# Attention steps between triples of the experts' products, with an order edge two steps back

## The chip, the cores and the metric

The kernel runs on one NeuronCore of a Trainium2 chip. The metric is the device time of one execution in microseconds (us); less is better. The engines are TensorE (PE in the rows; PEld is its loading of weights), VectorE (DVE), ScalarE (ACT), GpSimd (POOL) and SyncE (SP, which issues DMAs).

## What is computed

An attention over 2 x 8 heads of 576 positions and 64 features, with a causal mask and a bias from a running sum of `s`; then a mixture of four experts with dense weights (every token goes through every expert); then a gated layer. All of it is float32.

```python
def _attn_ref(q, k, v, s):                      # q, k, v: 2 x 8 x 576 x 64
    scores = np.matmul(q, k.transpose(0, 1, 3, 2)) / np.sqrt(D)
    cum = np.cumsum(np.maximum(s, 0.0), axis=-1)
    bias = -(cum[:, :, :, None] - cum[:, :, None, :])
    scores = np.where(causal, -1e9, scores + np.minimum(bias, 0.0))
    attn = np.exp(scores - np.max(scores, axis=-1, keepdims=True))
    attn = attn / (np.sum(attn, axis=-1, keepdims=True) + 1e-09)
    return np.matmul(attn, v)

def _moe_ref(x, domain_probs, w1, w2):          # x: 1152 x 512, four experts, F = 1024
    p = domain_probs / (domain_probs.sum(-1, keepdims=True) + 1e-09)
    for e in range(E):
        out += p[:, e:e + 1] * (np.maximum(x @ w1[e], 0.0) @ w2[e])

def _moe2_ref(x, w_a, w_b, w_out):              # F = 1536
    return ((x @ w_a) * (x @ w_b)) @ w_out
```

## The kernel before

Every float32 matrix is split into a high and a low part, and a product of two of them is a **triple** of matmuls, high x high, high x low and low x high, which the helper `mm3` (lines 255 to 261) issues to TensorE. All expert products therefore carry line 259 in the profile. An **attention step** works on the tiles of scores of 128 query rows: there are 80 such tiles in four groups (`GROUPS`: group 0 has 16 tiles, groups 1 and 2 have 24 each, group 3 has 16), and `attn_step` (line 792) is a software pipeline over them. In step n it issues, in this order, the transposes of tile n-3 (line 644), the score matmuls of tile n (lines 596 and 597), the normalisation of tile n-2 (ScalarE line 631, VectorE line 632, GpSimd line 633), the maximum and exponential of tile n-1 (VectorE line 606, ScalarE line 621), the P·V product of a head that is complete (line 680), and the evacuation of the transposes (ScalarE line 659 for the high part, VectorE line 661 for the low part). The first step of a head also prepares the next head (`prep_job`, among it the low half of k on GpSimd, line 564) and issues the loads of the head after that.

The work has three parts. First group 0 is done alone with the first weights being loaded (to about 38 us). Then `run(beside, True)` lays the experts' products of four stages beside the steps of groups 1 to 3: a stage is an expert and a range of 256 tokens, with eight first-layer units (`l1_unit`: four triples of 256 columns) and two second-layer units (`l2_unit`: eight triples of 512 columns); `pipelined` puts one first-layer unit of the next stage before the two second-layer units of a stage. Last, `run(after, False)` does the remaining experts and the gated layer without attention, with other pools of memory; its products write the tile psq.

What sets the order in the middle part: `run` keeps a clock `clock["t"]` of product time by a formula of the kernel, 3 x (columns / 2400 + 0.013) us for a triple, which is 0.36 us for 256 columns and 0.68 us for 512. After each unit it emits weight steps (a weight piece is loaded into `raw`, rounded by ScalarE at line 218 and its rest taken by GpSimd or VectorE at line 220) until their own clock has caught up, and then as many attention steps as the list `lead` asks for: steps 20 to 43 (group 1) in the first 29.7 us of product time, steps 44 to 67 in the next 22.35 us, steps 68 to 83 in the next 22.35 us; the last 15 us (`SLACK`) have none. Steps 0 to 19 have been emitted before the loop. The order on each engine is drawn from this program order at compile time: an instruction of lower place in the program goes first when a modelled run finds it ready; where it is not ready, a later one may pass it. On the chip each engine then takes its instructions in that order.

Of the kernel before, what the change touches and what calls it, by code (L numbers as in the profile page):

```python
# [19 lines left out]
P = 128  # L20
# [26 lines left out]
NT0 = 256  # L47

NFIRST = 4


@with_exitstack
def fused_kernel(ctx, tc, qT, kT, v, s, dp, w1, w2, wa, wb, wo, out):
    nc = tc.nc
# [13 lines left out]
    ident = const.tile([P, P], F32, name="ident")  # L68
# [3 lines left out]
    def split(hi, lo, src, lo_eng):  # L72
        nc.scalar.activation(out=hi, in_=src, func=AF.Copy)  # L73
        lo_eng.tensor_tensor(out=lo, in0=src, in1=hi.bitcast(F32), op=ALU.subtract)  # L74
# [117 lines left out]
    def split_piece(r, key, form, wide, src, j):  # L192
# [16 lines left out]
        else:  # L209
            nsplit[0] += 1  # L210
            lo_eng = nc.gpsimd if nsplit[0] % 2 or nsplit[0] <= NFIRST else nc.vector
            two = slice(2 * j, 2 * j + 2)
            if nsplit[0] <= NFIRST:
                nc.gpsimd.tensor_scalar(
# [37 lines left out]
    hts = {}  # L252
    begun = set()

    def mm3(ps, w, x, first, last, more=False):

        (lh, ll), (rh, rl) = w, x
        for k, (l, r) in enumerate(((lh, rh), (lh, rl), (ll, rh))):
            nc.tensor.matmul(  # L259
                ps, lhsT=l, rhs=r, start=first and k == 0, stop=last and k == 2, skip_group_check=more  # L260
            )

    def cols(pair, *at):
        return tuple(t[(slice(None), *at)] for t in pair)
# [316 lines left out]
    def st_enter(j, i):  # L581
        j.t[i] = Job()
        j.t[i].n = j.tiles[i][0] + P

    def st_scores(j, i):
        t = j.t[i]
        q0 = j.tiles[i][0] - j.q0
        cuts = [0, t.n] if t.n <= 512 else [0, 320, t.n]
        t.ps = []
        for c0, c1 in zip(cuts, cuts[1:]):  # L590
            ps = ps_s.tile([P, c1 - c0], F32, tag="sc", name=f"sc{j.nm}_{i}")
            t.ps.append((ps, c0, c1))
            if j.gi == 0:
                nc.tensor.matmul(ps, lhsT=j.qh[:, q0 : q0 + P], rhs=j.kr[:, c0:c1], start=True, stop=True)
                continue
            nc.tensor.matmul(ps, lhsT=j.qh[:, q0 : q0 + P], rhs=j.ks[:, c0:c1], start=True, stop=False)
            nc.tensor.matmul(ps, lhsT=j.qb[:, q0 : q0 + P], rhs=j.kb[:, c0:c1], start=False, stop=True)

    def st_softmax(j, i):
        t = j.t[i]  # L600
# [36 lines left out]
    def st_transpose(j, i):  # L637
        t = j.t[i]
        t.tp = []
        for c0, c1 in [(0, i + 1)] if i < 4 else [(0, 4), (4, 5)]:  # L640
            ps = ps_t.tile([P, c1 - c0, P], F32, tag="tr", name=f"tr{j.nm}_{i}")
            for c in range(c0, c1):
                k0 = j.tiles[c][0]
                nc.tensor.transpose(ps[:, c - c0, :], t.e[:, k0 : k0 + P], ident)  # L644
            t.tp.append((ps, c0, c1))

    def st_evac(j, i):
        t = j.t[i]
        if i == j.i0:

            j.eh = et_p.tile([P, j.i1, j.nr], F32R if j.gi else F32, tag="eh", name=f"eh{j.nm}")
            if j.gi:
                j.el = et_p.tile([P, j.i1, j.nr], F32R, tag="el", name=f"el{j.nm}")
        w0, r0, r1 = j.tiles[i]
        x = slice(r0 - j.r0, r1 - j.r0)
        for ps, c0, c1 in t.tp:
            src = ps[:, :, r0 - w0 : r1 - w0]
            hi = j.eh[:, c0:c1, x]
            nc.scalar.activation(out=hi, in_=src, func=AF.Copy)
            if j.gi:  # L660
                nc.vector.tensor_tensor(  # L661
                    out=j.el[:, c0:c1, x], in0=src, in1=hi.bitcast(F32), op=ALU.subtract
                )
        del j.t[i]
# [3 lines left out]
    def st_av(j):  # L668
        a = (j.h % 2) * D
        if j.gi == 0 and j.h % 2:  # L670
            ps = xpair[j.gi]
        else:
            ps = ps_a.tile([P, j.nr], F32, tag="av", name=f"av{j.nm}")
        mms = []
        for c in range(j.i1):
            o = max(0, j.tiles[c][1] - j.r0)
            for e in (j.eh, j.el) if j.gi else (j.eh,):
                mms.append((c, o, e))
        for m, (c, o, e) in enumerate(mms):
            nc.tensor.matmul(  # L680
                ps[:, o:] if j.gi else ps[a : a + D, o:],
                lhsT=j.vs[:, c, :],
                rhs=e[:, c, o:],
                start=(m == 0),
                stop=(m == len(mms) - 1),
            )
        c = D - a
        t0 = j.b * S + j.r0
        x = slice(t0, t0 + j.nr)
        if j.gi == 0:  # L690
            xpair[j.gi] = ps
            if j.h % 2:
                split(xh[j.h // 2][:, x], xl[j.h // 2][:, x], ps, nc.vector)
            return
        if j.h % 2 == 0:
            xpair[j.gi] = (
                x_p.tile([P, j.nr], F32, tag="xs", name="xs"),
                x_p.tile([P, j.nr], F32, tag="xt", name="xt"),
            )
        xs, xt = xpair[j.gi]  # L700
        nc.scalar.activation(out=xt[a : a + D, :], in_=ps[c : c + D, :], func=AF.Copy)
        nc.vector.tensor_tensor(  # L702
            out=xs[a : a + D, :], in0=ps[a : a + D, :], in1=xt[a : a + D, :], op=ALU.add
        )
        if j.h % 2 == 1:
            split(xh[j.h // 2][:, x], xl[j.h // 2][:, x], xs, nc.gpsimd)
# [8 lines left out]
    c0 = st_p.tile([NR, 1], F32, tag="c0", name="c0")  # L715
# [70 lines left out]
    state = {"n": 0}  # L786
    prep_job(jobs[0])

    def at(n):
        return seq[n] if 0 <= n < len(seq) else None  # L790

    def attn_step():
        n = state["n"]
        state["n"] += 1

        if x := at(n):
            j, i = x
            if i == j.i0:
                k = jobs.index(j)
                if k + 1 < len(jobs):  # L800
                    prep_job(jobs[k + 1])
                if k + 2 < len(jobs):
                    load_job(jobs[k + 2])
            st_enter(j, i)
        if x := at(n - 3):
            st_transpose(*x)
        if x := at(n):
            st_scores(*x)
        if x := at(n - 2):
            st_norm(*x)  # L810
        if x := at(n - 1):
            st_softmax(*x)
        if x := at(n - 4):
            j, i = x
            if i == j.i1 - 1:
                st_av(j)
        if x := at(n - 3):
            st_evac(*x)
        if x := at(n):
            j, i = x  # L820
            if i == j.i0:
                prep_v(j)
                k = jobs.index(j)
                if k + 1 < len(jobs):
                    load_v(jobs[k + 1])
# [6 lines left out]
    def close_attention():  # L832
        actx.close()
        open_pools(ctx, [("h2", 2), ("raw", 3), ("q", 2), ("cv", 1)])
        pools["late"] = True
        late_ps.append(ctx.enter_context(tc.tile_pool(name="ps_m2", bufs=5, space=PSUM)))
        for part_ in ("h", "l"):
            tq[part_] = ctx.enter_context(tc.tile_pool(name="tq" + part_, bufs=1)).tile(
                [P, 3, 2, SL], F32R, name="tq" + part_
            )  # L840
# [211 lines left out]
    n = [k for k, u in enumerate(after) if u[0] == ("w1", halves[1][1])][-1]  # L1052
# [11 lines left out]
    area = [0]  # L1064
# [5 lines left out]
    for n in (2, 3, 4):  # L1070
        us = sum(c for st in stages[:n] for part in expert_stage(*st) for _, c, _ in part)
        turn_t.append(us)
    SLACK = 15.0
    lead = []
    for g in range(3):
        u0 = lead[-1][1] if lead else 0.0
# [2 lines left out]
    PACE, LATE_PACE = 4.0, 3.0  # L1079
    clock = {"t": 0.0, "w": 0.0}  # L1080

    def run(units, attention):
        for k, cost, u in units:
            for key in keys_of(k):
                weights_to(key)
            u()
            for key in keys_of(k):
                used(key)
            if hold[0]:
                continue  # L1090
            clock["t"] += cost
            while clock["w"] < clock["t"]:
                clock["w"] += PACE if attention else LATE_PACE
                weight_step()
            if not attention:
                continue
            goal = state["n"]
            for u0, u1, s0, s1 in lead:
                if u0 < clock["t"]:
                    c = area[s0] + (area[s1] - area[s0]) * min(1.0, (clock["t"] - u0) / (u1 - u0))  # L1100
                    while goal < s1 and area[goal + 1] <= c + 1e-6:
                        goal += 1
            while state["n"] < goal:
                attn_step()

    run(beside, True)
    close_attention()
    run(after, False)


# [48 lines left out]
```

## Time and profile before

| | |
|---|---|
| Time, median of 3 runs | 761.77 us (760.43 to 764.9) |
| Time of the profiled execution | 760.76 us |
| Its span, from the first to the last instruction | 759.0 us |
| Mean granted clock of TensorE in it | 0.987 |
| TensorE busy | 719.9 us (95%) |
| VectorE busy | 533.0 us (70%) |
| GpSimd busy | 416.2 us (55%) |
| ScalarE busy | 334.8 us (44%) |

The times are of whole executions; the profile is one of them, taken by the hardware profiler, and all rows below are from it, in us from its first instruction. An engine's busy time is the union of its instructions' spans. A matmul's span includes its way through the array, so the next one starts before it ends: the distance between two starts is what a matmul costs, not its span. PEclk is the granted clock of TensorE as a share of the full one: 1.00 is 2.4 GHz and 0.50 is 1.2 GHz, and values between are means over a stretch.

### The profile page before, as it was taken

What the parts mean: (1) busy time and instruction counts of PE and PEld (TensorE: products, weight loads), DVE (VectorE), ACT (ScalarE), POOL (GpSimd) and SP (SyncE); (2) the same over time, 40 slices, a digit from 0 to 9 for tenths busy, and PEclk for the clock granted to TensorE, in tenths of its full rate; (3) what the DMA queues carried; (4) which work ended last, traced back from release to release, by engine and by line L of the source; (5) the groups of instructions that cost most, each with busy time, mean ns of one, the idle gap of its engine ahead of it and who ended that gap; (6) DMA issues with size and microseconds to landing.
All of it is one profiled execution on the core that took longest, in us unless ns stands there. A gap on an engine that the chain in (4) does not pass through costs nothing.

```text
span 759.0 us, 11106 instructions
## 1 busy us (share of the span) xinstructions
PE 719.9 (95%) x3868; PEld 630.9 (83%) x3868; DVE 533.0 (70%) x1119; ACT 334.8 (44%) x756; POOL 416.2 (55%) x330
## 2 busy tenths in 40 slices
PE   5979897997998999999999999999899999999997
PEld 3678886886978888888888888888788888898896
DVE  7656857757759777776556657679874788887764
ACT  4667748868864432223312323243645324242410
POOL 1777735647634754333313344598466878788600
PEclk9999998999998999999999999999999999999999
DMA  6457323324402131211001112122102132213003
GB/s 192 136 184 228 91 68 90 100 74 127 120 18 84 55 100 41 81 57 57 31 25 56 56 57 74 65 84 87 53 29 86 62 103 68 95 63 104 5 1 125
DMA packets 35095, 61.34 MB, mean 81 GB/s; under 512 B 3472, under 2 KB 19376, under 8 KB 35040
## 3 DMA queue, kind: packets, MB, share of 16 engines
q1 hardware_dynamic: 34864, 60.50, 24.8%
q8 instruction: 31, 0.51, 0.3%
q14 instruction: 24, 0.20, 0.1%
q10 hardware_dynamic: 176, 0.14, 0.1%
HBM read 55.02 MB, written 2.58 MB: 76 GB/s over the span
## 4 chain that ended last, share of the span: by engine, by line
PE 55%; DVE 12%; POOL 8%; issue 4%; ACT 2%; DMA 1%; POOLq 0%; ACTq 0%; DVEq 0%; SPq 0%
PE ps L259 27%; PE psq L259 20%; PE pst L259 4%; POOL wl L74 3%; PE av L680 2%; POOL tp L155 1%; DVE tp L167 1%; PE tr L644 1%; DVE tp L163 1%; DVE h2l L74 1%; DVE acc L1027 1%; DVE tp L159 1%; POOL t L155 1%; DVE t L167 1%; DVE psq L405 1%
## 5 line engine op out<-in xcount | busy, mean ns | idle before, releaser
L259 PE MATMUL ps<-wh,h2h 128*128 128x512 f32 x332 | 130.6, 393 | 0.0
L259 PE MATMUL ps<-wl,h2h 128*128 128x512 f32 x332 | 129.6, 390 | 0.0
L74 POOL TENSOR_TENSOR wl<-raw,wh 128x1024 fp32r<-128x1024 f32 x24 | 58.5, 2448 | 125.5 <-ACT wh L73 95.4
L259 PE MATMUL ps<-wh,h2l 128*128 128x512 f32 x332 | 125.7, 392 | 0.8 <-DVE h2l L74 0.8
L307 DVE SCALAR_TENSOR_TENSOR acc<-ps,pr,acc 128x512 f32<-128x512 f32 x111 | 82.1, 745 | 40.4 <-PE ps L259 39.7
L259 PE MATMUL psq<-xh,wh 128*128 128x448 f32 (+1 forms) x224 | 82.9, 372 | 1.7 <-DVE xs L702 1.7
L259 PE MATMUL psq<-xl,wh 128*128 128x448 f32 (+1 forms) x224 | 82.6, 369 | 0.0
L259 PE MATMUL psq<-xh,wl 128*128 128x448 f32 (+1 forms) x224 | 82.6, 370 | 0.0
L259 PEld LDWEIGHTS ps<-wh,h2l 128*128 128x128 f32 x332 | 62.2, 188 | 14.7 <-DVE h2l L74 1.6
L259 PEld LDWEIGHTS ps<-wh,h2h 128*128 128x128 f32 x332 | 62.4, 188 | 11.8 <-ACT h2h L73 0.3
L259 PEld LDWEIGHTS ps<-wl,h2h 128*128 128x128 f32 x332 | 62.4, 188 | 11.1
L318 ACT ACTIVATE h2h<-psq 128x448 fp32r<-128x448 f32 (+1 forms) x56 | 29.5, 532 | 93.6 <-PE psq L259 74.3
L74 POOL TENSOR_TENSOR wl<-sums,wh 128x1024 fp32r<-128x1024 f32 x24 | 58.6, 2441 | 5.2 <-ACT h2h L318 2.7
L73 ACT ACTIVATE wh<-raw 128x1024 fp32r<-128x1024 f32 x24 | 25.5, 1062 | 69.7 <-PE ps L259 52.9
L633 POOL TENSOR_SCALAR e<-e,r 128x448 f32<-128x448 f32 (+4 forms) x64 | 39.9, 630 | 28.9 <-DVE r L632 27.5
L259 PE MATMUL psq<-tqh,wh 128*128 128x448 f32 x144 | 52.9, 368 | 0.9 <-DVE h2l L74 0.5
L606 DVE CUSTOM_DVE_ANT_0 e<-sc,causal 128x128 f32<-128x128 f32 (+3 forms) x80 | 35.6, 450 | 24.2 <-PE tr L644 13.8
L259 PE MATMUL psq<-tql,wh 128*128 128x448 f32 x144 | 52.6, 365 | 0.0
L259 PE MATMUL psq<-tqh,wl 128*128 128x448 f32 x144 | 52.5, 364 | 0.0
L621 ACT ACTIVATE e<-e,mn 128x128 f32<-128x128 f32 (+4 forms) x80 | 45.9, 574 | 11.6 <-DVE mn L606 9.1
L644 PE MATMUL tr<-ident,e 128*128 128x128 f32 x240 | 45.2, 291 | 6.1 <-DVE el L661 4.1
L155 POOL TENSOR_SCALAR tp<-tp 128x512 f32<-128x512 f32 x24 | 47.4, 1995 | 5.9 <-ACT tp L154 5.9
(174 smaller groups left out, 1949.4 us busy)
## 6 DMA issues: line engine op xcount, KB each, us to landing
raw<-in_w SPq DMA_DIRECT2D x40, 512.0 KB
raw<-in_wa SPq DMA_DIRECT2D x12, 512.0 KB
raw<-in_wb SPq DMA_DIRECT2D x12, 512.0 KB
raw<-in_wo SPq DMA_DIRECT2D x12, 512.0 KB
kr<-in_kT SPq DMA_DIRECT2D x16, 288.0 KB
vr<-in_v SPq DMA_DIRECT2D x16, 160.0 KB
kb<-ks SPq DMA_DIRECT2D x16, 144.0 KB
out<-acc SPq DMA_DIRECT2D x9, 256.0 KB
```

The lines of the kernel that those rows point to most:

```text
L73: nc.scalar.activation(out=hi, in_=src, func=AF.Copy)
L74: lo_eng.tensor_tensor(out=lo, in0=src, in1=hi.bitcast(F32), op=ALU.subtract)
L155: nc.gpsimd.tensor_scalar(out=t.bitcast(F32), in0=t.bitcast(F32), scalar1=2.0**-15, scalar2=GMAX, op0=ALU.max, op1=ALU.min,)
L167: nc.vector.scalar_tensor_tensor(out=t, in0=hi, scalar=-(1 << 30), in1=t, op0=ALU.bitwise_and, op1=ALU.bitwise_or,)
L259: nc.tensor.matmul(ps, lhsT=l, rhs=r, start=first and k == 0, stop=last and k == 2, skip_group_check=more)
L307: nc.vector.scalar_tensor_tensor(out=dst, in0=ps, scalar=share, in1=dst, op0=ALU.mult, op1=ALU.add)
L318: nc.scalar.activation(out=hh, in_=src, func=AF.Relu)
L606: nc.vector.tensor_tensor_reduce(out=t.e[:, c0:c1], in0=ps, in1=causal[:, m0 + c0 : m0 + c1], scale=-1.0, scalar=seed, op0=ALU.add, op1=AL ...
L621: nc.scalar.activation(out=t.e, in_=t.e, func=AF.Exp, bias=mn, scale=-1.0 if j.gi else -SCALE, accum_out=t.l)
L633: (nc.gpsimd if j.gi else nc.vector).tensor_scalar(out=t.e, in0=t.e, scalar1=r, scalar2=1.0, op0=ALU.mult, op1=ALU.mult)
L644: nc.tensor.transpose(ps[:, c - c0, :], t.e[:, k0 : k0 + P], ident)
L680: nc.tensor.matmul(ps[:, o:] if j.gi else ps[a : a + D, o:], lhsT=j.vs[:, c, :], rhs=e[:, c, o:], start=(m == 0), stop=(m == len(mms) - 1),)
```

## The change

`mm3` gets two additions. After each triple of the middle part it calls `advance`, which adds the triple's own time to the clock and emits the attention steps that have fallen due; `run` no longer does this after the unit, and the weight steps stay where they were, after the unit. And the first matmul of each triple gets an edge behind the attention matmuls of the step `LAG` = 2 before the latest one emitted: the names of these (the last bias matmul of each score tile, the last transpose, the last P·V matmul) are kept in the list `passed`, one entry per step. The edge is of the kind NoSync: both ends are on TensorE, so it fixes their order in the queue and adds no semaphore. The first and the last part of the kernel are as before: there `mixed` is empty, and after the middle part `passed` is too.

```diff
+LAG = 2
...
+    passed, mixed = [], []
+    NOSYNC = mybir.DependencyInfo(mybir.DependencyClass.NoSync, mybir.DependencyReason.DATA)
+
     def mm3(ps, w, x, first, last, more=False):
 
         (lh, ll), (rh, rl) = w, x
         for k, (l, r) in enumerate(((lh, rh), (lh, rl), (ll, rh))):
-            nc.tensor.matmul(
+            ins = nc.tensor.matmul(
                 ps, lhsT=l, rhs=r, start=first and k == 0, stop=last and k == 2, skip_group_check=more
             )
+            if k == 0 and len(passed) > LAG:
+                for name in passed[-1 - LAG]:
+                    tc.add_manual_dep(ins.ins, name, NOSYNC, reason="the attention's pace")
+        if mixed:
+            mixed[0](3 * (rh.shape[-1] / 2400 + 0.013))
...
-            nc.tensor.matmul(ps, lhsT=j.qb[:, q0 : q0 + P], rhs=j.kb[:, c0:c1], start=False, stop=True)
+            ins = nc.tensor.matmul(ps, lhsT=j.qb[:, q0 : q0 + P], rhs=j.kb[:, c0:c1], start=False, stop=True)
+            passed[-1].append(ins.ins.name)
...
-                nc.tensor.transpose(ps[:, c - c0, :], t.e[:, k0 : k0 + P], ident)
+                ins = nc.tensor.transpose(ps[:, c - c0, :], t.e[:, k0 : k0 + P], ident)
             t.tp.append((ps, c0, c1))
+        passed[-1].append(ins.ins.name)
...
-            nc.tensor.matmul(
+            ins = nc.tensor.matmul(
                 ps[:, o:] if j.gi else ps[a : a + D, o:],
...
+        passed[-1].append(ins.ins.name)
...
     def attn_step():
         n = state["n"]
         state["n"] += 1
+        passed.append([])
...
+    def advance(us):
+
+        clock["t"] += us
+        goal = state["n"]
+        for u0, u1, s0, s1 in lead:
+            if u0 < clock["t"]:
+                c = area[s0] + (area[s1] - area[s0]) * min(1.0, (clock["t"] - u0) / (u1 - u0))
+                while goal < s1 and area[goal + 1] <= c + 1e-6:
+                    goal += 1
+        while state["n"] < goal:
+            attn_step()
+
     def run(units, attention):
...
-            clock["t"] += cost
+            if not attention:
+                clock["t"] += cost
             while clock["w"] < clock["t"]:
                 clock["w"] += PACE if attention else LATE_PACE
                 weight_step()
-            if not attention:
-                continue
-            goal = state["n"]
-            for u0, u1, s0, s1 in lead:
-                if u0 < clock["t"]:
-                    c = area[s0] + (area[s1] - area[s0]) * min(1.0, (clock["t"] - u0) / (u1 - u0))
-                    while goal < s1 and area[goal + 1] <= c + 1e-6:
-                        goal += 1
-            while state["n"] < goal:
-                attn_step()
-
+
+    mixed.append(advance)
     run(beside, True)
+    mixed.clear()
+    passed.clear()
     close_attention()
     run(after, False)
```

## Rows read from the trace of the kernel before

**Rows 1.** Page, part 1: busy us, share of the span, instructions.

```profile
PE 719.9 (95%) x3868; PEld 630.9 (83%) x3868; DVE 533.0 (70%) x1119; ACT 334.8 (44%) x756; POOL 416.2 (55%) x330
```

**Rows 2.** Stretches: length; busy us (instructions) by engine; PEclk, DMA share, GB/s.

```profile
56.00:112.00 56.00, 53.88 (x346) 48.85 (x345) 39.48 (x108) 38.77 (x105) 35.48 (x36) 1.00 0.44 138
112.00:139.00 27.00, 21.91 (x134) 19.15 (x132) 19.13 (x64) 21.58 (x75) 14.46 (x22) 0.87 0.29 83
139.00:172.00 33.00, 32.90 (x225) 30.07 (x224) 21.85 (x84) 23.80 (x90) 17.68 (x30) 1.00 0.30 85
172.00:191.00 19.00, 13.64 (x93) 11.23 (x92) 14.18 (x48) 16.27 (x50) 14.55 (x17) 1.00 0.48 134
191.00:221.00 30.00, 30.00 (x207) 27.58 (x205) 19.93 (x62) 22.10 (x64) 15.64 (x19) 1.00 0.28 78
221.00:231.60 10.60, 6.92 (x51) 5.60 (x49) 6.63 (x15) 4.94 (x13) 2.35 (x3) 0.96 0.06 16
231.60:759.00 527.40, 519.17 (x2620) 456.45 (x2620) 374.50 (x597) 176.80 (x278) 284.94 (x165) 0.99 0.19 65
```

**Rows 3.** The same for line 259 alone, the products: PE, PEld, PEclk, DMA.

```profile
112.00:139.00 27.00, 3.00 (x22) 2.58 (x20) 0.87 0.29 83
139.00:172.00 33.00, 23.95 (x134) 19.09 (x132) 1.00 0.30 85
172.00:191.00 19.00, 2.78 (x18) 2.33 (x18) 1.00 0.48 134
```

**Rows 4.** Waits of TensorE from 112 to 139 us: total us, times, longest.

```profile
PE tr L644 <- DVE el L661: 2.8, 3, 1.4
```

**Rows 5.** Timeline of TensorE near 105 us: start, us, instruction.

```profile
101.12 0.40 PE L259 MATMUL ps<-wh,hh 128*128 128x512 f32 x1
101.35 0.40 PE L259 MATMUL ps<-wl,hh 128*128 128x512 f32 x1
...
104.06 0.62 PE L644 MATMUL tr<-ident,e 128*128 128x128 f32 x4
104.43 0.39 PE L596 MATMUL sc<-ks,qh 128*128 128x320 f32 x1
...
109.46 0.28 PE L259 MATMUL ps<-xl,wh 128*128 128x256 f32 x1
109.58 0.28 PE L259 MATMUL ps<-xh,wl 128*128 128x256 f32 x1
```

**Rows 6.** Stretches around 237.6 us, all engines, columns as in rows 2.

```profile
230.80:237.60 6.80, 6.01 (x19) 6.01 (x20) 6.74 (x13) 0.70 (x2) 0.73 (x1) 0.50 0.71 230
237.60:244.40 6.80, 6.80 (x39) 6.54 (x38) 6.77 (x14) 4.73 (x9) 5.47 (x2) 1.00 0.02 5
```

**Rows 7.** Weight splits, line 220: DVE and POOL by stretch; a wait of ScalarE.

```profile
38.00:56.00 18.00, 4.13 (x4) 8.76 (x7) 0.91 0.55 172
56.00:112.00 56.00, 7.74 (x8) 9.85 (x8) 1.00 0.44 138
112.00:231.60 119.60, 0.00 (x0) 0.00 (x0) 0.97 0.30 84
...
ACT wh L218 <- DMA raw<-in_w: 8.7, 5, 3.9
```

**Rows 8.** Products (L259) from 20 to 49.9 us; timeline of TensorE after them.

```profile
20.00:49.90 29.90, 14.58 (x84) 12.51 (x84) 0.94 0.43 132
...
49.92 0.32 PE L596 MATMUL sc<-ks,qh 128*128 128x320 f32 x1
...
54.69 0.38 PE L259 MATMUL ps<-xh,wh 128*128 128x256 f32 x1 [2.72 <-DVE hl L287]
```

**Rows 9.** Exponentials (L621) by stretch, two records each: ACT, PEclk, DMA.

```profile
112.00:139.00 27.00, 8.16 (x26) 0.87 0.29 83
139.00:172.00 33.00, 7.67 (x28) 1.00 0.30 85
172.00:191.00 19.00, 6.24 (x16) 1.00 0.48 134
```

## The prediction

> **What bounds the kernel now.** The page's busy shares come first [rows 1]: TensorE is busy 95% of the span and no other engine passes 70%. That share says too much, because a matmul's span in the trace is longer than the time until the next one starts. So the second view is the table of stretches [rows 2]. I cut the part in which attention and expert products run together, from 38 us to the last P·V product at 231.6 us, where the character of the work changes, and there are two kinds of stretch. From 139 to 172 and from 191 to 221 us TensorE has no idle time to speak of and the clock is at 1.00. From 112 to 139, from 172 to 191 and from 221 to 231.6 us it is busy 21.91 of 27.00, 13.64 of 19.00 and 6.92 of 10.60 us, and in the first of these the granted clock falls to 0.87. After 231.6 us it is busy to 98%, and nothing of that phase is edited.
>
> The third view counts the products (L259) in the first two of these poor stretches [rows 3]: 22 and 18 matmuls, while TensorE ran 134 and 93 in all. So they are attention almost alone. ScalarE, on the other hand, is busy 21.58 of 27.00 and 16.27 of 19.00 us there [rows 2], and the longest of TensorE's waits in the first of them is for the low half of a transposed tile, which VectorE makes from what ScalarE has evacuated [rows 4]. In a burst the attention runs at the pace of its chain over ScalarE, VectorE and GpSimd, and no product stands behind the late matmul in TensorE's order to fill the gap.
>
> Where the bursts come from is in the code: the loop `run` lays attention steps behind a whole unit. A first-layer unit is four triples, 1.44 us by the kernel's own formula, a second-layer unit is eight triples or 5.43 us. A step falls due every 1.16 us of product (64 steps in the 74.4 us that `lead` covers), so two second-layer units in a row leave nine steps in a heap.
>
> **What the triples and steps cost, in slots.** From start to start of neighbours [rows 5], a 512-column product takes 0.23 us, a 256-column one 0.12, and four transposes 0.37. Scores and P·V products move 128 to 448 columns, by proportion 0.06 to 0.20 us, so I take 0.125 us as the mean for a matmul of attention, an estimate from these rows. With it the work in the three poor stretches is: 22 x 0.12 + 112 x 0.125 = 16.6 us of 27.0; 18 x 0.12 + 75 x 0.125 = 11.5 of 19.0; and in the last one, with hardly a product, 51 x 0.125 = 6.4 of 10.6. The unused time is 10.4 + 7.5 + 4.2 = 22.1 us. To this comes the clock behind the last one: 19 matmuls in 6.80 us at 0.50 against 39 in the 6.80 us after it at 1.00 [rows 6], which is 3.3 us of work lost. That makes 25.4 us: **the change can win about 25 us**, and only in these places.
>
> **The change, part by part.** (1) The pacing moves into `mm3`: after every triple the clock advances by 0.36 or 0.68 us of product and at most one or two steps are emitted, where up to five were. The number of instructions on every engine stays the same, DMA issues included. A step that is emitted earlier also comes earlier, against the weight pieces that still follow a unit, in the queues of SP (three loads of q, k and bias rows, one of v, one copy of the rounded k per head) and of GpSimd (the low halves of k and v, the scaling by 1/sum). The sum of issues is the same, and I put this at nothing, because all weight pieces of this phase are split before 112 us, none after it [rows 7], while the steps that move are mostly later; a weight piece that came late would cost a wait like the 2.72 us of [rows 8].
>
> (2) What mixing is worth. Per step TensorE would have 1.16 us of product and about 1.1 us of attention (112 x 0.125 us over the 13 steps of the first poor stretch, 75 x 0.125 over the 8 of the second), 2.3 us. The attention alone, in the bursts, needs (27.0 - 2.6) / 13 = 1.9 and (19.0 - 2.2) / 8 = 2.1 us a step; the steps are counted by the exponentials, each of which leaves two records on ScalarE, 26 and 16 here [rows 9]. So over the whole phase TensorE becomes the later one, but with a margin of 10 to 20% only. In the second group (tiles of 128 to 320 rows of keys) the sides change: 22.35 us of product over 24 steps is 0.93 us, with the attention of the stretch from 139 to 172 us, (225 - 134) x 0.125 / 14 = 0.8 us [rows 2, 3, 9], 1.75 us a step against 1.9. There TensorE will still wait 0.15 us a step, **3.6 us** that I take off the 25. The bounds are 0 (the chain keeps up, as in that stretch, which has no gap) and 24 x (2.1 - 1.75) = 8.4 us.
>
> (3) The order edge. The first matmul of each triple stands behind the matmuls of the attention step two back. It adds no semaphore, but TensorE runs its queue in order: behind a score or transpose that still waits stand all later triples, and behind these the ReLU evacuation on ScalarE and VectorE and the weight slabs' release. Today products may run far ahead, and at the start they do: 84 product matmuls, 28 triples, ran before the score at 49.92 us [rows 8], which is that of step 19 and is followed by step 20's. The loop's first step is 20; step 22 falls due after 4 us of product, and from there each triple stands behind step 20's matmuls. So only some 9 to 11 triples may pass ahead of these scores. If they stay where they are, 17 to 19 triples of 0.36 us, up to 6.8 us, are pushed behind them. Part finds room in the 2.72 us gap before 54.69 us [rows 8]; and if the scores come as soon as their operands are there, less is lost. Bounds 0 and 6.8, taken **3.5 us**, the middle, since half of it fits into that gap.
>
> (4) The weight pieces. Before 112 us, 18.6 us of splitting on GpSimd (15 instructions), 11.9 on VectorE (12) and 8.7 us in which ScalarE waits for raw weights [rows 7], 39 us in all, stand between attention instructions on engines that take them in order. With the products tied to the attention they can hold TensorE more often than now. It loses 2.1 us by its idle time from 56 to 112 us today [rows 2]; I take another **2 us**, with bounds 0 and the whole 39, near the low end, because 16 of the 27 splits and most of the first group's steps passed in that stretch with 2.1 us idle.
>
> **The sum.** 25.4 - 3.6 - 3.5 - 2.0 = 16 us. The profiled execution has a span of 759.0 us in a time of 760.76, so 743 and 744.8 us; the median of the runs is 1.0 us above the profiled one, which gives **746 us**.
>
> **Rivals.**
> (a) Full mixing: none of the three deductions comes, and 761.8 - 25 = 737 us. For it speak the two stretches with no idle time at all, where attention was mixed in; against it that there were two to three parts of product to one of attention in them, and half and half is planned now. Chance 0.16.
> (b) Slower: the edge makes one queue of two. The late instruction is a score, transpose or P·V product whose input stands behind a weight piece on GpSimd, VectorE or ScalarE; triples may be only two steps, 2.3 us, ahead, and two splits in a row on GpSimd take 2.5 us. If two thirds of the 39 us in (4) came to hold TensorE, 26 us, with the 3.5 of the start and the 3.6 of the second group, the time is 762 - 25 + 33 = 770 us. It decides from 18 us of the 39 onwards. Against it: TensorE's idle time in that stretch is 2.1 us although attention matmuls are in its order there too. Chance 0.16.
> (c) The change does not do what it says: TensorE's order is drawn at compile time by readiness and program order, and it may come out with the same heaps, for the edge forbids products ahead of attention but not attention in a heap. Then 760 us. Against it: no more than two steps are emitted between two triples now, so the heap has no source. Chance 0.10.
> (d) The clock. In the trace the mixed stretches are granted 1.00 and the attention alone 0.87 [rows 2]. If the half-and-half mix were granted 0.87 throughout, its 64 x 2.3 = 147 us of work would take 0.13 x 147 = 19 us longer, 765 us. Chance 0.04. The Trainium skill ("Perfetto Trace Analysis", section Matmul Optimizations) speaks for this rival: TensorE's power follows its use, so matmuls should run back to back in batches, and this change cuts batches up. The trace does not agree so far: its batches of attention are where the clock fell.
>
> **How the numbers follow.** My own case has 0.54. A measurement of this kernel can tell about 0.5%, 3.8 us, from no change. Faster by more holds my case and (a): 0.70. Within 0.5% either way lie (c) and (d): 0.14. Slower is (b): 0.16. The range leaves out (b) and (d), 0.20, and goes from (a) with its rounding to (c) with some room: 735 to 762 us. The bounds of the deductions lie in it: with all of them at nothing it is 737, with (2) and (3) at their upper ends 754.
>
> **What would show it.** Right: idle time and half clock of TensorE near 112, 172 and 221 us shrink; product matmuls per stretch become even; the last P·V product lies some 10 us before the last expert product, so TensorE is busy and at full clock when the late phase begins, at about 216 us instead of 231.6. Step (3): a new gap between 40 and 50 us. Step (2): small waits for VectorE and ScalarE in the second group. Rival (b) shows as gaps of 2 us and more between 40 and 110 us that end with attention matmuls. The forecast is wrong if the phase before the last P·V product does not shorten, or if the late phase loses what it gains.

## The result and the profile after

The changed kernel takes 750.45 us in the median (748.68 to 755.17, 4 runs) against 761.1 us (758.53 to 764.9, 4 runs) for the kernel before: a ratio of 0.987, 95% interval 0.982 to 0.992. The spans of the two profiled executions are 748.7 and 759.0 us, 10.3 us apart. The forecast was 746 us: right in direction, with 16 us promised where 10 came.

The busy times of the page, as in [rows 1]: TensorE 8.6 us less, every other engine within 3 us.

```profile
PE 711.3 (95%) x3868; PEld 624.1 (83%) x3868; DVE 532.7 (71%) x1119; ACT 335.3 (45%) x756; POOL 413.4 (55%) x330
```

So the work is the same and lies elsewhere. The stretches of the changed kernel, in the columns of [rows 2], where those of before stand, except for 38 to 56 us.

```profile
38.00:56.00 18.00, 12.51 (x81) 11.53 (x80) 13.77 (x33) 14.25 (x36) 17.43 (x16) 0.88 0.64 209
56.00:112.00 56.00, 47.68 (x323) 43.18 (x322) 42.01 (x118) 42.04 (x113) 37.85 (x40) 0.99 0.45 131
112.00:139.00 27.00, 25.86 (x186) 23.66 (x186) 21.52 (x84) 25.37 (x99) 18.00 (x30) 1.00 0.39 107
139.00:172.00 33.00, 32.82 (x240) 30.75 (x239) 24.84 (x87) 28.97 (x95) 22.93 (x30) 1.00 0.47 125
172.00:191.00 19.00, 19.00 (x117) 16.79 (x116) 11.78 (x38) 11.90 (x35) 9.54 (x12) 1.00 0.37 103
191.00:221.00 30.00, 28.52 (x205) 26.48 (x204) 21.50 (x54) 16.31 (x46) 9.68 (x12) 1.00 0.22 69
221.00:231.60 10.60, 10.60 (x59) 10.09 (x58) 10.57 (x18) 4.26 (x9) 2.39 (x2) 1.00 0.01 2
...
223.80:748.70 524.90, 515.16 (x2621) 452.27 (x2619) 366.69 (x585) 175.84 (x275) 280.16 (x164) 1.00 0.20 62
```

From 112 us on the three poor stretches are gone: TensorE is busy 25.86 of 27 us where it was 21.91, 19.00 of 19 where it was 13.64, 10.60 of 10.60 where it was 6.92, and the clock is at 1.00 throughout. Before 112 us it is the other way round: 47.68 of 56 where it was 53.88. The products (line 264 now) are spread, 80, 125 and 55 matmuls in the stretches that had 22, 134 and 18 [rows 3]:

```profile
112.00:139.00 27.00, 14.50 (x80) 11.29 (x81) 1.00 0.39 107
139.00:172.00 33.00, 21.57 (x125) 17.51 (x124) 1.00 0.47 125
172.00:191.00 19.00, 12.96 (x55) 9.18 (x53) 1.00 0.37 103
```

The late phase (first product into psq) begins at 223.80 us instead of 231.59, 7.8 us sooner (start, us, instruction; first before, then after):

```profile
231.59 0.69 PE L259 MATMUL psq<-xh,wh 128*128 128x384 f32 x1 [1.71 <-DVE xs L702]
```

```profile
223.80 0.34 PE L264 MATMUL psq<-xh,wh 128*128 128x384 f32 x1
```

The last P·V product starts at 213.71 us, ten before the last expert product, so this seam has no half clock any more; the two rows answer to [rows 6]:

```profile
230.80:237.60 6.80, 6.80 (x35) 6.10 (x34) 4.46 (x8) 3.61 (x6) 5.32 (x3) 1.00 0.04 9
237.60:244.40 6.80, 6.80 (x35) 6.18 (x35) 3.95 (x8) 0.98 (x2) 0.61 (x1) 1.00 0.20 72
```

From there to the end it is 524.9 us instead of 527.45, 2.6 us less. 7.8 and 2.6 are the whole gain.

**A ledger of TensorE's lost slots.** For each matmul I took the distance from its start to the next start, less a fixed price for its kind (about columns / 2.4 ns plus 11 to 14 ns, 109 ns for a transpose, which is its most frequent distance), and added it up by stretch. Idle time, half clock and slow starts all fall into it. In us:

| | 20 to 38 | 38 to 56 | 56 to 112 | 112 to the late phase | sum | late phase begins |
|---|---|---|---|---|---|---|
| before | 9.0 | 7.0 | 3.8 | 28.4 | 48.2 | 231.6 |
| after | 11.7 | 8.5 | 11.9 | 8.4 | 40.5 | 223.8 |

The sums differ by 7.7 us, as the beginnings of the late phase do (7.8): the same matmuls stand before it in both kernels. So the change won **20.0 us after 112 us and lost 12.3 us before it**. What made the gain, and what the loss, is what the experiments are about.

In the part that lost, from 38 to 112 us, TensorE had these waits, 13.7 of its 13.8 us of idle time (us in all, times, longest):

```profile
PE tr L655 <- DVE el L673: 5.6, 3, 2.0
PE sc L606 <- DVE mn L617: 3.0, 3, 1.5
PE sc L606 <- POOL ks L574: 2.6, 1, 2.6
PE sc L607 <- DMA kb<-ks: 1.3, 1, 1.3
PE tr L655 <- DVE mn L617: 1.2, 1, 1.2
```

All five end with a score or a transpose, none with a product, so no product waited for its own weights there, and behind each hold stood products that could have run. The third one by its timeline (start, us, engine, line, instruction, in brackets the idle time before it and its releaser):

```profile
36.57 2.10 ACT L220 ACTIVATE wh<-raw 128x1024 fp32r<-128x1024 f32 x2
...
37.70 5.90 POOL L222 TENSOR_TENSOR wl<-raw,wh 128x512 fp32r<-128x512 f32 x4 [4.41 <-ACT wh L220]
43.67 1.60 POOL L574 TENSOR_TENSOR ks<-kr,ks 64x576 fp32r<-64x576 f32 x1
...
45.32 0.41 PE L606 MATMUL sc<-ks,qh 128*128 128x320 f32 x1 [2.60 <-POOL ks L574]
```

GpSimd works 5.90 us on four low halves of weights, then makes the low half of k, and only then the score can start. In the kernel before, products ran in such times.

### The profile page after: what moved, and what is told of

Its sections match the earlier page's. It is cut to its first block, busy times and chain, and to the rows that moved or that the text cites. A ratio compares the mean times of both kernels' runs of the same rounds, so it can differ in the third digit from the quotient of the medians.

```text
span 748.7 us, 11078 instructions
## 1 busy us (share of the span) xinstructions
PE 711.3 (95%) x3868; PEld 624.1 (83%) x3868; DVE 532.7 (71%) x1119; ACT 335.3 (45%) x756; POOL 413.4 (55%) x330
## 4 chain that ended last, share of the span: by engine, by line
PE 59%; DVE 15%; POOL 9%; ACT 6%; issue 6%; DMA 4%; SPq 0%; POOLq 0%; ACTq 0%; DVEq 0%
PE ps L264 29%; PE psq L264 20%; PE pst L264 4%; POOL wl L76 3%; PE av L692 2%; PE tr L655 2%; DMA kr<-in_kT 2%; PE sc L604 1%; ACT e L632 1%; POOL tp L157 1%; DMA raw<-in_w 1%; DVE tp L169 1%; DVE tp L165 1%; DVE h2l L76 1%; ACT wh L220 1%
## 5 line engine op out<-in xcount | busy, mean ns | idle before, releaser
L644 POOL TENSOR_SCALAR e<-e,r 128x448 f32<-128x448 f32 (+4 forms) x64 | 37.9, 596 | 25.1 <-DVE r L643 23.1
L673 DVE TENSOR_TENSOR el<-tr,eh 128x512 fp32r<-128x512 f32 (+5 forms) x80 | 38.5, 483 | 16.1 <-ACT eh L671 15.4
L415 DVE TENSOR_TENSOR u<-psq,s 128x448 f32<-128x448 f32 x48 | 29.6, 618 | 28.4 <-PE psq L264 22.3
```

Of the source, the lines that this page charges most:

```text
L415: nc.vector.tensor_tensor(out=out, in0=a, in1=b, op=ALU.add)
L644: (nc.gpsimd if j.gi else nc.vector).tensor_scalar(out=t.e, in0=t.e, scalar1=r, scalar2=1.0, op0=ALU.mult, op1=ALU.mult)
L673: nc.vector.tensor_tensor(out=j.el[:, c0:c1, x], in0=src, in1=hi.bitcast(F32), op=ALU.subtract)
```

## The experiments

All ratios are against the kernel before on the same chip (medians there 759.0 to 760.6 us). "Begins" is the start of the late phase in the profiled execution, one for each kernel; the first run below shows that it can differ by 0.9 us between two executions of one order.

### Which half of the change works

Theory M: laying the steps between triples (the mixing) wins, the edge only costs. Theory E: the edge wins, because it keeps the attention from falling behind the products.

**Emission per triple without the edge.**

```diff
-LAG = 2
+LAG = 1000
```

> The changed kernel without its order edges: steps are emitted after each triple, nothing ties a triple to them. Theory M (mixing wins, the edge only costs by holding products while attention stands behind weight pieces): 740 to 747 us, the changed kernel's 8.3 us of idle TensorE from 56 to 112 us falls below 4. Theory E (the edge is what keeps attention from falling behind): 756 to 762 us, with attention alone again at the end of the phase. If both halves matter, 748 to 753.

Measured: 759.4 us, ratio 1.0006 (0.9984 to 1.0028); it begins at 232.5. Laid side by side with the kernel before, the compiled order is the same on all five engines, instruction for instruction (3868 matmuls on TensorE, 1119 instructions on VectorE, 756 on ScalarE, 330 on GpSimd, and all DMA issues of SyncE). So the grain of the emission alone changes nothing here: the order drawn at compile time was already free of it. The poor stretches are all there, and since the program is the same, the small differences from [rows 2] are those of one execution from another:

```profile
112.00:139.00 27.00, 22.66 (x141) 19.68 (x140) 19.78 (x73) 22.48 (x79) 15.22 (x23) 0.90 0.30 83
172.00:191.00 19.00, 15.12 (x91) 12.74 (x90) 13.73 (x47) 15.90 (x48) 14.13 (x16) 0.91 0.46 128
```

**The edge without the mixing.** Steps are emitted after the unit as before, in one go; the edges stay.

```diff
             if hold[0]:
                 continue
-            if not attention:
-                clock["t"] += cost
+            clock["t"] += cost
             while clock["w"] < clock["t"]:
                 clock["w"] += PACE if attention else LATE_PACE
                 weight_step()
+            if attention:
+                advance(0.0)
...
-    mixed.append(advance)
     run(beside, True)
```

> The edge with steps emitted after whole units, as before the change. Theory M: no gain or a loss, 760 to 770 us, because up to five steps are laid in a heap and the next triple must stand behind all but the last two of them. Theory E: 748 to 754 us.

Measured: 763.0 us, ratio 1.0034 (1.0002 to 1.0066); it begins at 235.8. The ledger has 35.7 us up to 112 and 16.8 after it: the early loss is 3.6 us larger than in the changed kernel, the gain after it 11.6 us instead of 20.0. After a heap of steps has been emitted, the next triple stands behind all of it but the last two, so the heaps of the code should now be in TensorE's order, with the products between them; one stretch with idle time and less clock is back, others are full (first row against 32.82 us and 1.00 in the changed kernel):

```profile
139.00:172.00 33.00, 28.95 (x172) 25.33 (x171) 20.74 (x81) 25.39 (x91) 19.27 (x29) 0.90 0.37 99
172.00:191.00 19.00, 19.00 (x138) 17.91 (x138) 11.83 (x36) 13.83 (x39) 10.55 (x12) 1.00 0.40 111
```

By their times, the first run fell where theory E had put it (756 to 762 us) and this one where theory M had put it (760 to 770), so neither half wins by itself. M's claim that mixing alone wins falls. The edge makes the gain after 112 us, but it wins only with steps that are emitted singly, so that it binds product by product.

**Where the heaps came from.** Products (line 259, 264) and exponentials (line 621, 632; two records a tile) up to 112 us, kernel before and then after; busy us (count):

```profile
0.00:112.00 112.00, 56.21 (x298) 45.77 (x299) 0.98 0.49 152
0.00:112.00 112.00, 23.22 (x72) 0.98 0.49 152
```

```profile
0.00:112.00 112.00, 35.22 (x195) 29.39 (x195) 0.94 0.52 157
0.00:112.00 112.00, 25.47 (x78) 0.94 0.52 157
```

Before, 298 product matmuls had run by then, 45.9 us on the kernel's own clock. By that clock the rule of `lead`, which weighs a step by the columns of its tile, has emitted 64 steps, and the exponentials of 36 tiles had run: the attention was **28 steps behind** the pace that the program asked for (one of them is the pipeline's own). It falls behind all the time, 8 steps at 50 us, 12 at 80, 28 at 112, and the bursts that I took for heaps of the emission are it catching up: 16 behind at 139, 14 at 172, 8 at 191. In the changed kernel 195 matmuls (28.5 us, 42 steps) and 39 tiles make 3 behind at 112, and counted at every microsecond from 40 us on it is never more than 4 behind.

### How tight, and from where

**Four steps instead of two, and one** (`LAG = 4`, `LAG = 1`).

> The changed kernel with the edge four steps back instead of two. Theory M: the holds between 38 and 112 us get shorter, 744 to 749 us. Theory E: the attention runs later behind the products, 751 to 757 us.

> The changed kernel with the edge one step back. Without the edge the compiled order on every engine was that of the kernel before, instruction for instruction, so the edge alone draws the order. If what counts is that products are held back evenly, 746 to 753 us; if a tight edge turns the attention's latency into holds of TensorE, 754 to 765 us with more waits of TensorE for VectorE and ScalarE.

Measured: with four 756.4 us, ratio 0.9959 (0.9926 to 0.9993), begins at 226.1; with one 750.7 us, ratio 0.9879 (0.9855 to 0.9904), begins at 225.2. The ledger of four has 35.1 us up to 112 and 7.7 after it; of one, 35.7 and 6.2. Four lies in theory E's range: a looser edge did not give back what was lost early. One step is as good as two.

**The edge only from a later step on** (44, then 30 steps emitted, counted from the first step of the kernel; the first edges then go to steps 42 and 28, not 46 and 32 as the two texts below say).

```diff
-            if k == 0 and len(passed) > LAG:
+            if k == 0 and len(passed) > 44:
```

> The changed kernel with the edge from step 46 on alone, that is after the weight pieces of this phase. Theory M: the holds before 112 us go, 741 to 747 us. Theory E: the first group falls behind, 751 to 758 us.

> The changed kernel with the edge from step 32 on alone. With the edge from 46 on the time was that of the edge from the start, so the first 26 steps' edges won and lost nothing on balance. If that holds for any start before the second group: 749 to 752 us. If the edge in the weight stretch costs (theory W) and helps once most pieces are split: 743 to 748 us.

Measured: 750.24 us, ratio 0.9871 (0.9842 to 0.9901), begins at 224.0; and with 30, 751.5 us, ratio 0.9882 (0.9858 to 0.9906), begins at 227.4. In both, products run early as in the kernel before (the first at 22.6 and 22.5 us, against 37.6 with the edge from the start), and it gains nothing: the ledgers to 112 us come to 30.4 and 35.9 us, beside 32.1. The first time lies in neither theory's range, the second where it was put if the start does not matter (its profile is of the longest of its four executions, 754.3 us). What is not held early is held once, later. The run from 44 has a stretch of attention alone until it has caught up; all of TensorE first, then the products alone:

```profile
88.00:121.00 33.00, 26.42 (x149) 21.28 (x149) 25.04 (x86) 28.14 (x90) 21.31 (x28) 0.90 0.36 101
```

```profile
88.00:121.00 33.00, 0.00 (x0) 0.00 (x0) 0.90 0.36 101
```

So the early holds are not a cost of where the edge begins. By 112 us 38 to 39 tiles are done in each of the six kernels with the edge, and 36 before: up to there the attention's pace hardly depends on the edge, and the next runs ask what sets it.

### What holds the attention before 112 us

Theory W: the weight pieces of this stretch stand between the attention's instructions on ScalarE, VectorE and GpSimd. Rival A: it is the attention's own chain.

**The weight pieces taken away**, in the kernel before and in the changed one. All weight slabs of the middle part are one pair of zeroed tiles; left out are their loads and splits, so that the products of the first expert stages are zero.

```diff
+    zero = new_slab()
+    for t in zero:
+        nc.vector.memset(t.bitcast(F32), 0.0)
...
-                queue((key, w), "slab", src[w])
+                slabs[key, w] = zero
+                kind_of[key, w] = "slab"
+                live["slab"] += 1
```

> The kernel before with no weight work in the middle part: the eight slabs of the first two experts are one pair of zeroed tiles, so their loads, roundings and splits are left out and the products run on zeros. Theory W (weight pieces between attention instructions are what holds TensorE in the changed kernel before 112 us): little to gain here, 752 to 757 us, mainly the 2.7 us gap near 52 us. Rival A (the attention's own chain sets the pace of the first group): the same 752 to 757 us.

> The changed kernel with the same weight work left out. Theory W: the holds of 1.3 to 2.6 us between 38 and 105 us vanish, 735 to 741 us, some 16 us below the kernel before with the same left out. Rival A: they stay, 744 to 748 us, 9 to 11 us below it, as with the weights.

Measured: 754.4 us, ratio 0.9943 (0.9921 to 0.9966), and 741.6 us, ratio 0.9759 (0.9711 to 0.9807), which is 0.6 us above W's range. The totals understate it, since the late phase is 8 us longer in both (535.4 and 533.4 us). In the second, TensorE waits 3.5 and 2.0 us at its start for ReLU halves that VectorE and ScalarE make; what delays these was not followed. The four executions of the second took 738.0, 738.3, 744.8 and 744.9 us, and the profile, with what is read from it here, is of the one of 738.3; what the other 6.5 us are is open. By the beginning of the late phase, 216.4 and 203.15 us, the pieces cost the kernel before 15.2 us and the changed one 20.7; without them the change is worth 13.3 us there instead of 7.8. Where they cost it is in the ledger:

| | up to 112 | 112 to the late phase | sum |
|---|---|---|---|
| before | 19.8 | 28.4 | 48.2 |
| before, no weight pieces | 11.6 | 21.0 | 32.6 |
| after | 32.1 | 8.4 | 40.5 |
| after, no weight pieces | 14.2 | 5.2 | 19.4 |

TensorE from 38 to 112 us, the kernel before and the same without the pieces:

```profile
38.00:112.00 74.00, 67.67 (x436) 61.57 (x437) 49.58 (x133) 49.96 (x132) 49.49 (x47) 0.98 0.47 146
```

```profile
38.00:112.00 74.00, 73.86 (x505) 67.78 (x504) 46.31 (x149) 49.42 (x153) 34.69 (x42) 1.00 0.28 75
```

Then the changed kernel and the same without the pieces:

```profile
38.00:112.00 74.00, 60.18 (x402) 54.71 (x400) 55.78 (x150) 56.29 (x149) 55.28 (x55) 0.96 0.50 150
```

```profile
38.00:112.00 74.00, 72.95 (x538) 68.72 (x537) 55.54 (x190) 62.63 (x201) 43.44 (x59) 1.00 0.35 95
```

In the changed kernel 13.8 us of idle time become 1.05, with 538 matmuls in the stretch instead of 402, and 52 tiles are done by 112 us instead of 39. W holds. That the products run on zeros is not what saves the time: at 1.00 they start 0.12 us (256 columns) and 0.23 us (512) apart with and without the pieces. In the kernel before, the pieces cost 8.2 us on the spot, and 7.4 us later: they put the attention behind, TensorE ran products meanwhile, and the bill came as bursts after 112 us. But 21.0 of the 28.4 us after 112 us stay without them, and the attention is then still 23 steps behind at 112 us: in the kernel before it falls behind mostly for other reasons than the pieces. With the edge there is no such credit: 17.9 us on the spot, 3.2 later. And without the pieces the edge itself loses 2.6 us early (14.2 against 11.6).

**Loads or splits.** Two pairs of runs keep one half of the pieces' work. With the loads alone, the slab products take zeroed tiles as above, and the high and low halves are left out. With the splits alone, every split works on one raw piece, and the other loads are left out, so the products take wrong weights; that piece has one of the three raw buffers to itself.

Loads alone:

```diff
-            slabs[key] = place_of(form)
+            slabs[key] = zero if form == "slab" else place_of(form)
...
+        if form == "slab":
+            return
         wh, wl = slabs[key]
```

Splits alone:

```diff
+        if form == "slab" and raw0:
+            return raw0[0]
```

> The changed kernel; the weight slabs of the middle part are loaded as before, piece by piece, but not split: their products take one pair of zeroed slabs. Left out: the high and low halves of these slabs (lines 220 and 222), so the expert products of the first stages are zero. It stands against the run without loads and splits, whose late phase began at 203.1 us from the start, where that of the changed kernel began at 223.8: 20.7 us are the weight pieces' price. Theory S (the split instructions hold TensorE: ScalarE, VectorE and GpSimd take them in order between attention instructions, and products wait for the slabs): with the loads alone the late phase begins at 203 to 206 us, and the span is about 737 to 742 us. Theory D (the transfers: q, k and v rows and the copies of k come later because raw weights lie before them in the queue and on the DMA engines): it begins at 216 us or later.

> The same edit on the kernel before (weight slabs of the middle part loaded, not split; left out: their high and low halves). Its late phase began at 231.6 us, without loads and splits at 216.4. Theory S: 216 to 219 us. Theory D: 227 us or later.

> The changed kernel; every split instruction of the weight slabs is issued, but on one raw piece that is loaded once: the other loads of the middle part's slabs are left out (so the expert products of the first stages take wrong weights). Theory S: the late phase begins at 219 to 224 us, since the instructions are all there. Theory D: at 203 to 208 us. If both halves cost something, ScalarE's waiting for raw weights (8.7 us in the kernel before) being the part that the loads carry, this one begins at about 215 us and the one with loads alone at about 211.

> The same edit on the kernel before (all splits issued on one raw piece; the other loads of the middle part's slabs left out). Theory S: the late phase begins at 229 to 232 us. Theory D: at 216 to 219 us.

| | late phase begins: all pieces | loads alone | splits alone | none | ratio, loads alone | ratio, splits alone |
|---|---|---|---|---|---|---|
| before | 231.6 | 219.2 | 230.8 | 216.4 | 0.997 (0.995 to 0.999) | 1.002 (1.001 to 1.004) |
| after | 223.8 | 210.1 | 224.7 | 203.15 | 0.979 (0.977 to 0.981) | 0.988 (0.985 to 0.991) |

The splits alone cost all of it (14.4 and 21.6 us), the loads alone 2.8 and 7.0; the two overlap. (The profile of the splits alone in the kernel before is of its shortest execution, 759.1 us in a median of 762.9.) So theory S holds for the price, with an addition that it had not: loads alone cost the changed kernel 7.0 us, beyond the 3 that S allowed. Some of both lies before 38 us; from there to the late phase the changed kernel's ledger has 28.8 us with all pieces, 27.7 with the splits alone, 13.3 with the loads alone and 9.7 with none. One hold of that kind is in the changed kernel at 85.75 us, where ScalarE waits for a row of q, the high half of a transposed tile is queued behind that, and TensorE waits for its low half:

```profile
75.67 0.79 DVE L568 SCALAR_TENSOR_TENSOR qb<-qr,qh 64x384 fp32r<-64x384 f32 x1
...
76.49 0.34 SPq L557 DMA_DIRECT2D qr<-in_qT  x1
...
81.37 0.53 ACT L567 ACTIVATE qh<-qr 128x384 fp32r<-128x384 f32 x1 [2.09 <-DMA qr<-in_qT]
...
84.38 0.60 ACT L671 ACTIVATE eh<-tr 128x512 fp32r<-128x512 f32 x1
...
85.75 0.33 PE L655 MATMUL tr<-ident,e 128*128 128x128 f32 x1 [1.98 <-DVE el L673]
```

SyncE's queue did not hold this q: it was issued at 76.49 us, when VectorE had just read the row before out of the buffer (75.67 to 76.46), and ScalarE started 4.9 us later. What part of these the two weight pieces issued at 72.68 us have, by their transfers on the DMA engines, was not told apart. No run was faster than the changed kernel with its whole work done: one step of lag and the edge from step 44 on are equal to it within their intervals.

## Why the prediction was right, and where it was not

**The gross gain: right, and its places too.** After 112 us the prediction counted 22.1 us and took 3.6 off for step (2), 18.5 net; the ledger shows 20.0. Of the 3.3 us for the half clock at the seam (3.5 by its own rows: 20 of 39 matmuls short in 6.80 us), 2.6 came. The stretches, the even products and the last P·V product are as "what would show it" said; the late phase begins at 223.8 us and not at 216.

**Step (1), the mixing at nothing: right in price, wrong in cause.** It said that the bursts come from heaps that the loop emits after a unit. The run without the edge shows that the emission decides nothing: same order on five engines. What makes the bursts is the rule that the document had quoted of the kernel, that a later instruction may pass one that is not ready: products pass the attention where it is late, by 28 steps at 112 us, and it catches up alone. The rows for this were in the trace before: 298 product matmuls and 72 exponential records by 112 us, to be set beside the pace in `lead`. With this went the argument against **rival (c)**: "the heap has no source" was wrong, and (c) is just what half of the change does by itself. The edge, entered as a cost only, is what won, together with the mixing. So that the sum had the right sign was in part luck: the mixing, to which the prediction gave the whole gain, wins nothing without the edge.

**Step (2), 3.6 us in the second group: right, a little large.** The second group's exponentials run from 103.6 to 142 us in the changed kernel, and the waits of TensorE in that time are 1.5, 0.4, 0.3 and 0.2 us, 2.4 in all. The 20.0 us above are net of them, but for the 1.5, which ends before 112 us.

**Step (3), the early hold, 3.5 us: near in size, as 2.6 us, but by luck.** The size is that of the run without weight pieces, where nothing else holds. By stretches it is 1.0 us more up to 38 us, 1.1 less up to 56 and 2.7 more up to 112; the prediction had put it between 40 and 50 us. In the changed kernel, the gap that came there, 2.60 us at 45 us, is behind weight pieces. What the edge itself holds comes earlier, since the prediction overlooked that 20 steps stand in `passed` when the first triple is issued, so that this triple is tied to step 17. In TensorE's order, the first product stands right behind that step's last score:

```profile
37.26 0.57 PE L607 MATMUL sc<-kb,qb 67*128 67x448 f32 x1
37.63 0.41 PE L264 MATMUL ps<-xh,wh 128*128 128x256 f32 x1
```

Before, the first product starts at 22.8 us. 46 product matmuls are done by 49.9 us instead of 84 [rows 8], and TensorE, with the attention alone up to 37.6 us, gets half the clock for ten microseconds, where it had 1.00 (ten us each, first before, then after):

```profile
30.00:40.00 10.00, 8.57 (x50) 6.01 (x48) 6.88 (x23) 7.08 (x22) 5.64 (x6) 1.00 0.38 121
```

```profile
30.00:40.00 10.00, 9.44 (x35) 6.46 (x35) 6.94 (x17) 5.52 (x14) 5.50 (x5) 0.50 0.51 169
```

Up to 38 us the ledger has 11.7 us instead of 9.0. Starting the edge later gives these back, but the time does not fall, as the runs from 44 and from 30 show.

**Step (4), the weight pieces, 2 us: this is the term that failed.** They hold TensorE for 17.9 us before 112 us where it was 8.2, 9.7 us more instead of 2. The prediction's bounds, 0 and 39, held it; the value was taken near the low end because TensorE idled only 2.1 us in that stretch before. That row did not show what it was taken for: TensorE was not idle because it ran products ahead on credit, and the change ends the credit. The waits that came were named, in rival (b), and are there: 2.60 us behind four low halves of weights on GpSimd, 1.93 us behind two on VectorE, after which comes the low half of a transposed tile, and 1.98 us behind the late q. The second of these:

```profile
94.89 3.15 DVE L222 TENSOR_TENSOR wl<-raw,wh 128x512 fp32r<-128x512 f32 x2
...
97.96 0.68 DVE L673 TENSOR_TENSOR el<-tr,eh 128x512 fp32r<-128x512 f32 x1
...
98.78 0.52 PE L655 MATMUL tr<-ident,e 128*128 128x128 f32 x3 [1.93 <-DVE el L673]
```

So (b) had the mechanism, and its 9.7 us are less than the 18 us at which it would have decided.

With the measured terms the sum reads 20.0 + 2.6 - 2.6 - 9.7 = 10.3 us, the difference of the two spans: after 112 us, the seam, step (3) and step (4).

**Rivals (a) and (d).** Without the weight pieces the middle part gains 13.3 us and not 20 and more, so full mixing was out of reach also for another reason: of the 28.4 us of bursts, 7.4 were the pieces' own. For (d), the half-and-half mix was granted 1.00 from 112 us on, so it did not come. Attention alone was granted 0.90 in the run with the edge from 44 and 0.50 from 30 to 37.6 us here, but 1.00 from 172 to 191 us in the kernel before [rows 2], with 5.36 us idle (0.91 in the run without the edge, which has the same order). So the prediction's word that the batches of attention are where the clock fell holds for some of them only. The Trainium skill ("Perfetto Trace Analysis", section Matmul Optimizations) wants matmuls back to back in batches. These runs agree in part: the mixed stream with hardly a gap kept 1.00, but one stretch with many gaps kept it too.

## What to carry to other kernels

Where the order of two streams is drawn from readiness, compare how far each has come with the pace that the program sets, at several times: a stream that falls behind shows as bursts much later. Here finer emission alone did not mend it, and an order edge did once the steps were emitted singly. Before such an edge is priced, ask what the engine ran during the waits of the stream that it ties to: an idle time near zero there may be credit, and the holds that it covers come due in full (here 8 us became 18).

## What was not expected of the hardware

The clock fell to 0.50 in the changed kernel from 30 to 40 us although TensorE was busy 9.44 of those 10 us; what came ahead of it is a stretch with 2.32 us busy in 4.00, at 1.00:

```profile
26.00:30.00 4.00, 2.32 (x14) 1.46 (x13) 3.59 (x17) 3.47 (x13) 3.92 (x4) 1.00 0.34 96
```

In the kernel before, TensorE was busy for all of these 4.00 us, and without the weight pieces the changed kernel was granted 1.00 from 30 to 40 us. So the busier of two stretches can be the one at half the speed. The count of matmuls hints at it, 35 in these 10 us against 50 in the same ten of the kernel before, and the distance between like matmuls shows it: 0.21 us for 256 columns here, 0.12 at full clock [rows 5].

```profile
38.70 0.41 PE L264 MATMUL ps<-xh,wl 128*128 128x256 f32 x1
38.91 0.41 PE L264 MATMUL ps<-xh,wh 128*128 128x256 f32 x1
```
